# Transposed loads, zeroing by DMA, accumulator copies on VectorE and a split return of reciprocals in a fused attention and state-space kernel

## The chip, the core and the metric

The kernel runs on one core of a Trainium2 chip. The metric is the device time of one execution in microseconds, as the median of several runs. The span in a profile is the time from the first to the last instruction of one profiled execution, which is a little shorter.

## What is computed

Two branches over the same token count (2048) and width (448), mixed by a gate. Only one input, `A_x`, feeds both.

```python
g = sigmoid((x * gate_w).sum(-1))                 # one gate per token
# branch A: attention, 16 query heads of 28, one shared key/value head
q, k, v = x @ wq, x @ wk, x @ wv
a = (softmax(q @ k.T / sqrt(28)) @ v) @ wo
# branch B: diagonal state space, 256 complex states per channel, as a long convolution
dt = exp(log_dt); A = A_re + 1j*A_im
K[d, l] = Re( sum_n C[d, n] * exp(dt*A[d, n]*l) * dt*B[d, n] )
b = causal_conv(x, K) + x * Dskip                 # per channel, by FFT in the reference
out = g * a + (1 - g) * b
```

Inputs and output are bfloat16.

## The kernel before

Every operation is recorded first by `Prog.op` (L99) or `Prog.dma` (L134), with an engine, an assumed duration in ns, the keys it reads and writes, and a priority `pr` (lower is more urgent). `Prog.schedule` (L148) then simulates the engines with these durations and writes down one fixed order for each engine; `emit` (L257) turns the keys into semaphore waits. So a changed duration, priority or dependency moves instructions on all engines, and each engine follows its order strictly: whatever stands behind a waiting instruction waits too. `fill` (L624) adds matmuls that multiply by zero wherever the order leaves TensorE idle, to keep its clock up.

**Head.** `loads` (L487) brings x in four quarters of 512 tokens (`lx`, L492), six parameter arrays as raw rows (`lraw`, L499), and the weights, nearly all from the queue of SyncE. In `prep_x` (L553) TensorE transposes each quarter in two halves (L565), ScalarE evicts one half (L574) and VectorE the other (L576); the keys follow (L582), are copied by ScalarE (L588), and VectorE takes their largest magnitude (L591). The maximum over all four quarters (L602) goes into a bound `Wb` (L604) that the query projection uses (`qproj`, L806, with its second product at L825 and its copy at L828), so no score can be computed before the last quarter has come through. `prep_params` (L712) transposes the parameters on TensorE (`trans`, L732) and turns them into seeds of the state tables with VectorE (L750 to L756) and ScalarE (sines at L757 and L758, exponentials at L762 and L764). `sload` (L793) moves the first block's seeds to `sz` and `sw` by DMA. Contractions over the 448 columns of x are cut into four pieces of 112 partitions.

**Body.** `main` (L1162) walks through 1024 score tiles of 128 keys by 512 queries, in sets of three and two in turn. For each set TensorE computes scores (`qk`, L1181), ScalarE takes the exponential of the whole set (L1205) into a ring of 15 tiles, and two sets later TensorE multiplies four tiles with the values (`pv`, L1214) into one PSUM bank, `psB`. After 64 tiles a group of four heads for 512 queries is complete: `norm` (L1066) copies the bank to `acc` on ScalarE (L1074; the last two groups on VectorE), which frees it for the next group. GpSimd then moves the 2048 denominators to `denT` (L1080), VectorE inverts them (L1082), GpSimd writes them to a scratch tensor (L1085) and reads them back broadcast over the partitions into `rdenB` (L1086), and VectorE multiplies (L1088).

Between these, for branch B, VectorE squares "master" powers (`masters`, L831) and builds tables from them (`tables`, L876), TensorE contracts them to the convolution kernel (`kgen`, L938, matmuls at L959), and GpSimd stores it (slots `kw0` and `kw1`). SyncE loads it back as Toeplitz tiles of 1072 KB (`tload`, L991), and TensorE convolves (`conv`, L1000, matmuls at L1015, inverse transforms at L1037), adding into the output buffer `O` (L1045). There are 28 convolutions and 112 such loads.

**Tail.** After the last exponential the last group is normalised with matmuls instead of DMA (L1091 onwards) and `tail` (L1124) makes the last output tiles and stores everything.

Of the kernel before, what the change touches and what calls it, by code (L numbers as in the profile page):

```python
# [11 lines left out]
P = 128  # L12
# [19 lines left out]
HALVES = (13,)  # L32
NTR = 5
# [47 lines left out]
class Prog:  # L81
# [52 lines left out]
    def dma(self, pairs, desc, slot, rd=(), wr=(), pr=0, eng="sp", slow=False, extra=0):  # L134
        kw = dict(allow_slow_non_contiguous=True) if slow else {}

        def fn(e):
            return [e.dma_start(o, i, **kw) for o, i in pairs]  # L138
        nd, size = desc
        o = self.op(eng, fn, nd * (30.0 + 0.03 * size if size < 1500 else 105.0 + 0.022 * size) / 16.0 * 1.1, rd, wr, pr)  # L140
        o.slot, o.ndma, o.extra = slot, len(pairs), extra
        prev = self.slots.get(slot)
        if prev is not None:
            o.deps[prev] = 1
        self.slots[slot] = o.i
        return o
# [210 lines left out]
class Kernel:  # L357
# [18 lines left out]
    def build(self):  # L376
        nc = self.nc
        with self.es:
            self.pg = Prog(nc, self.es)
            self.alloc()  # L380
            self.consts()
            self.loads()
            self.prep_x()
            self.prep_params()
            self.prep_gate()
            self.main()
            self.pg.schedule()
            self.fill()
            with nc.Block() as block:
                self.pg.emit(block)  # L390

    def alloc(self):
# [26 lines left out]
        self.tslots = [(self.T, s * TW, ["tpdone", "rawdone"]) for s in range(NTR)]  # L419
# [26 lines left out]
    def consts(self):  # L446
# [13 lines left out]
        dm(self.Wq.v(0, P, 28, [[32, 64], [1, 4]]), 0.0, 300, ["Wq"])  # L460
# [22 lines left out]
        dm(V(self.Wo, 0, NT * D), 0.0, 810, ["Wo"], 5)  # L483
        for q in range(4):
            dm(V(self.O, q * 4 * D, 4 * D), 0.0, 800, [("O", q)], 5)

    def loads(self):  # L487
# [4 lines left out]
        def lx(q):  # L492
            pg.dma([(self.xst.v(0, P, q * 4 * D, [[1, 4 * D]]), dram(x, q * 4 * P * D, [[4 * D, P], [1, 4 * D]]))],
                   (128, 3584), f"x{q}", wr=[("xst", q)])
# [4 lines left out]
        def lraw(k):  # L499
            pg.dma([(raw.v(0, DT, k * 1024, [[1, 1024]]), dram(ins[names[k]], 0, [[1024, DT], [1, 1024]]))],  # L500
                   (112, 2048), f"raw{k}", wr=[("raw", k)])
# [3 lines left out]
        pg.dma([(self.dtb.v(0, P, 0, [[1, D]]), dram(ins["B_log_dt"], 0, [[0, P], [1, D]]))], (128, 896), "ldt", wr=["dt"], eng="act")  # L505
        lx(0)
        lraw(0)
        for k, (w, n) in enumerate((("A_wk", DH), ("A_wv", DH), ("gate_w", 1))):
            pg.dma([(wks.v(0, DT, 112 * k, [[n, 4], [1, n]]), dram(ins[w], 0, [[n, DT], [DT * n, 4], [1, n]]))],
                   (448, 2 * n), f"wk{k}", wr=[("wks", k)], eng="act", slow=True)  # L510
        for q in range(1, 4):
            lx(q)
        pg.dma([(wst.v(0, DT, 0, [[D, 4], [1, D]]), dram(ins["A_wq"], 0, [[D, DT], [DT * D, 4], [1, D]]))],
               (448, 896), "wq", wr=["wqs"])
        lraw(1)
        pg.op("dve", lambda e: e.tensor_copy(self.Wk.v(0, DT, 0, [[32, 16], [1, DH]]),
                                             wks.v(0, DT, 0, [[DH, 4], [0, 4], [1, DH]])), 300, rd=[("wks", 0)], wr=["Wk"], pr=-0.6)
        pg.op("dve", lambda e: e.tensor_copy(self.Wq.v(0, DT, 0, [[32, 64], [1, DH]]),
                                             wst.v(0, DT, 0, [[DH, 64], [1, DH]])), 620, rd=["wqs"], wr=["Wq"], pr=-0.5)
        pg.op("dve", lambda e: e.tensor_copy(self.Wv.v(0, DT, 0, [[32, 4], [1, DH]]), wks.v(0, DT, 112, [[DH, 4], [1, DH]])),  # L520
              180, rd=[("wks", 1)], wr=["Wv"], pr=0.1)
        pg.op("dve", lambda e: e.tensor_copy(self.Wv.v(0, DT, 28, [[32, 4]]), wks.v(0, DT, 224, [[1, 4]])),
              100, rd=[("wks", 2)], wr=["Wvg"], pr=0.1)
        rs = self.U.rs
        for k, (h, p0, b0) in enumerate(((1, 16, 15), (0, 0, 15), (1, 0, 31))):
            ap = bass.AP(tensor=self.U.h, offset=h * rs + p0 * D, ap=[[2 * rs, 64], [D, 16], [1, D]])
            pg.dma([(ap, dram(x, 64 * b0 * D, [[D, 64], [-64 * D, 16], [1, D]]))],
                   (1024, 896), f"u{k}", rd=["Uz"] if p0 else [], wr=[("U", k)], pr=0.5)
        for k in range(2, 6):
            lraw(k)  # L530
        pg.dma([(self.skt.v(32 * g + 31, 1, 0, [[8, 14], [1, 8]]), dram(ins["B_Dskip"], 8 * g, [[16 * D, 1], [32, 14], [1, 8]]))
                for g in range(4)], (112, 8), "sk", rd=["skt"], wr=["skt"], pr=1, slow=True)
        w = ins["A_wo"]
        pg.dma([(self.Wo.v(32 * r, DH, 0, [[D, 4], [1, D]]), dram(w, DH * r * D, [[D, DH], [4 * DH * D, 4], [1, D]]))
                for r in range(4)], (448, 896), "wo", rd=["Wo"], wr=["Wo"], pr=2)
        pg.dma([(dram(self.KP, KH + 1024, [[4 * KW, 112], [KW, 4], [1, 64]]), self.kstg.v(0, 112, 0, [[64, 4], [1, 64]]))],
               (448, 128), "pad", rd=[("kst", 0, 0), ("kst", 1, 0)], wr=["pad"], pr=3)
# [15 lines left out]
    def prep_x(self):  # L553
        pg = self.pg
        xst, xT, kT = self.xst, self.xT, self.kT
        sm = self.small
        for q in range(4):
            for hp in range(2):
# [3 lines left out]
                def mm(e, q=q, hp=hp, t=t, o=o):  # L562
                    for Tl in range(2):
                        for k in range(4):
                            r = e.matmul(t.v(0, DT, o + 512 * Tl + 128 * k, [[1, 128]]),  # L565
                                         xst.v(0, P, (4 * q + k) * D + (2 * hp + Tl) * DT, [[1, DT]]),
# [3 lines left out]
                dst = xT.v(0, DT, 2048 * q + 1024 * hp, [[512, 2], [4, 128], [1, 4]])  # L570
                src = t.v(0, DT, o, [[512, 2], [1, 128], [128, 4]])
# [5 lines left out]
            b = 4  # L577
            t, o = self.bank(b)

            def mk(e, q=q, t=t, o=o):  # L580
                for T in range(NT):
                    r = e.matmul(t.v(0, P, o, [[1, 512]]), self.Wk.v(0, DT, T * P, [[1, P]]),  # L582
                                 xT.v(0, DT, 2048 * q + 512 * T, [[1, 512]]),
# [11 lines left out]
            def mv(e, q=q):  # L595
                for kt in range(4 * q, 4 * q + 4):
                    for T in range(NT):
                        r = e.matmul(self.psB.v(0, P, 32 * kt, [[1, 29]]), xT.v(0, DT, 2048 * q + 512 * T + 128 * (kt - 4 * q), [[1, 128]]),
                                     self.Wv.v(0, DT, T * 32, [[1, 29]]), start=(T == 0), stop=(T == 3), tile_position=(0, 0))
                return r  # L600
            pg.op("pe", mv, 900, rd=["Wv", "Wvg"] + self.xk(q), wr=[("b", 6)], pr=0.5)
# [12 lines left out]
              rd=[("b", 6), "vz"], wr=["gt"], pr=0.4)  # L614
# [97 lines left out]
    def prep_params(self):  # L712
# [7 lines left out]
        tt = lambda j: spot[j][0].v(0, P, spot[j][1], [[D, 2], [4, DT], [1, 4]])  # L720
        tc = lambda j: spot[j][0].v(0, P, spot[j][1], [[D, 2], [16, 2 * NC], [1, 16]])
        K = lambda j: ("tp", j)
        dtb = self.dtb.v(0, P, 0, [[0, 2], [4, DT], [1, 4]])
# [3 lines left out]
        dtp2 = self.rdenB.v(0, P, 0, [[0, 2], [4, DT], [1, 4]])  # L727
        pg.op("act", lambda e: e.activation(dtf, d1, AF.Exp), 600, rd=["dt"], wr=[("acc", 0)], pr=-1)
        pg.op("dve", lambda e: e.tensor_copy(d1, dtf), 300, rd=[("acc", 0)], wr=["dt"], pr=-0.4)
        pg.op("dve", lambda e: e.tensor_scalar(dtp, d1, 1.0 / TWO_PI, None, ALU.mult), 300, rd=["dt"], wr=["rd"], pr=-0.4)  # L730

        def trans(k, pr):  # L732
            t_ = self.grp()
            X = ("rx", k)

            def mm(e):
                for half in range(2):
                    for T in range(4):
                        r = e.matmul(t_.bv(0, P, half * D + DT * T, [[1, DT]]),
                                     raw.v(0, DT, k * 1024 + T * NM + 128 * half, [[1, 128]]),  # L740
                                     self.ident.v(0, DT, 0, [[1, DT]]), is_transpose=True, tile_position=(0, 0))
                return r
            pg.op("pe", mm, 700, rd=[("raw", k), "id"], wr=[X, "rawdone"], pr=pr, lock=t_)
            return t_, X
# [3 lines left out]
        def vt(o, a, b, op, rd, wr, pr, **kw):  # L748
            f = lambda a: a.bv(0, P, 0, [[D, 2], [1, DT], [DT, 4]]) if isinstance(a, Grp) else a
            pg.op("dve", lambda e: e.tensor_tensor(o, f(a), b, op), ns, rd=rd, wr=wr, pr=pr, **kw)  # L750
        p0, k0 = trans(0, -0.4)
        vt(tt(1), p0, dtp2, ALU.mult, [k0, "rd"], [K(1)], -0.4, unlock=p0)
        pg.op("dve", lambda e: e.tensor_scalar(t(2), t(1), MAGIC, None, ALU.add), 660, rd=[K(1)], wr=[K(2)], pr=-0.4)
        pg.op("dve", lambda e: e.scalar_tensor_tensor(t(1), t(2), -MAGIC, t(1), ALU.add, ALU.subtract), ns,
              rd=[K(1), K(2)], wr=[K(1)], pr=-0.4)
        pg.op("dve", lambda e: e.scalar_tensor_tensor(t(2), t(1), -1.0, t(1), ALU.mult, ALU.max), ns, rd=[K(1)], wr=[K(2)], pr=-0.4)  # L756
# [3 lines left out]
        p1, k1 = trans(1, 0.15)  # L760
        vt(tt(0), p1, dtb, ALU.mult, [k1, "dt"], [K(0)], 0.2, unlock=p1)
        pg.op("act", lambda e: e.activation(t(5), t(0), AF.Exp), 2230, rd=[K(0)], wr=[K(5)], pr=0.5)  # L762
# [537 lines left out]
```

## Time and profile before

| what | value |
|---|---|
| time, median of 3 runs | 541.87 us (540.47 to 544.5) |
| span of the profiled execution | 539.0 us |
| first exponential starts | 26.74 us |
| last exponential ends | 527.73 us |
| exponentials | 410 instructions, ScalarE |
| copies of `psB` on ScalarE | 14 |
| copies of `psB` on VectorE | 1 whole (L1076), 2 halves (L1095) |
| Toeplitz loads | 112 of 1072 KB, 11.0 us from issue to landing |

In the profile, PE is TensorE's matmuls, PEld its weight loads, DVE VectorE, ACT ScalarE, POOL GpSimd and SP SyncE. A line of the groups gives code line, engine, operation, what is written from what, shapes and count; then busy time and the mean of one; then idle time of the engine just ahead of them, with what ended it. `<-` in a DMA line reads "destination from source". The clock is TensorE's, 1.00 at full speed.

### The profile page before, as it was taken

To read this page: it belongs to the slowest core of one execution; us is meant where nothing else is said; L and a number is where in the kernel's file an instruction comes from. 1 tells how busy PE (TensorE), PEld (TensorE's weight loads), DVE (VectorE), ACT (ScalarE), POOL (GpSimd) and SP (SyncE) were. 2 spreads that over 40 slices of the span, in tenths; PEclk is the share of its full clock that TensorE was granted. 3 is DMA by queue.
4 is the path that set the end of the run, shared out by engine and by line. 5 is a ranking of instruction groups with operands and counts; after the bars stand their busy time and mean duration, and the time that the engine had idled before them with its cause. 6 is when DMAs were issued, how large, how long until landed. Compare 5 with 4: busy or idle time off the path is not lost.

```text
span 539.0 us, 20180 instructions
## 1 busy us (share of the span) xinstructions
PE 486.4 (90%) x9186; PEld 249.5 (46%) x9186; DVE 449.5 (83%) x891; ACT 497.5 (92%) x458; POOL 102.1 (19%) x192
## 2 busy tenths in 40 slices
PE   7698999989999899888999898989999898999887
PEld 4442233235454555353555454553556355644434
DVE  7979999989999999899999999999999695331203
ACT  3799999998999999989999999999999796899992
POOL 2000002200431404012040430040042213220000
PEclk9989999998999999999999999999999796899998
DMA  8931100793398987979778989999859997999722
GB/s 235 283 121 47 37 21 7 251 347 116 118 376 300 329 358 284 351 259 386 296 240 363 327 273 348 400 351 367 343 191 356 353 380 287 348 344 392 261 88 71
DMA packets 39042, 142.89 MB, mean 265 GB/s; under 512 B 11240, under 2 KB 22032, under 8 KB 24620
## 3 DMA queue, kind: packets, MB, share of 16 engines
q1 hardware_dynamic: 28316, 135.30, 69.0%
q0 software_dynamic: 9104, 6.13, 4.4%
q8 instruction: 72, 1.18, 0.9%
q10 hardware_dynamic: 1536, 0.17, 0.3%
q14 instruction: 14, 0.11, 0.1%
HBM read 135.39 MB, written 5.74 MB: 262 GB/s over the span
## 4 chain that ended last, share of the span: by engine, by line
ACT 56%; PE 26%; DMA 8%; DVE 8%; issue 2%; ACTq 0%
ACT expT L1205 54%; PE psS L1181 7%; PE psB L1214 4%; PE psS L959 3%; PE psX L959 3%; DMA rdenB<-R_scratch 3%; PE psX L1015 3%; DMA denT<-acc 2%; DMA sz<-in_A_wv_dram 2%; PE psS L1015 2%; ACT acc L1074 1%; DMA R_scratch<-denT 1%; DVE msq L856 1%; DVE xT L576 1%; DVE tab L911 1%
## 5 line engine op out<-in xcount | busy, mean ns | idle before, releaser
L1205 ACT ACTIVATE expT<-psS 128x1536 bf16<-128x1536 f32 (+1 forms) x410 | 470.6, 1340 | 18.7 <-PE psS L1181 11.7
L1181 PE MATMUL psS<-qT,kT 32*128 32x512 bf16 x1024 | 164.3, 395 | 29.8 <-ACT expT L1205 22.3
L1214 PE MATMUL psB<-expT,vaug 128*32 128x512 bf16 x1024 | 105.1, 400 | 3.7 <-issue 3.2
L1181 PEld LDWEIGHTS psS<-qT,kT 32*128 32x128 bf16 x1024 | 39.5, 91 | 119.3 <-ACT expT L1205 97.3
L1187 PE MATMUL psB<-ident,zero 32*128 32x512 bf16 x190 | 74.9, 394 | 0.0
L911 DVE TENSOR_TENSOR tab<-tab,mbf 128x256 bf16<-128x256 bf16 (+5 forms) x75 | 69.6, 928 | 1.2
L1015 PE MATMUL psX<-T,U 128*18 128x128 bf16 (+7 forms) x1920 | 54.7, 243 | 4.2 <-issue 3.2
L1214 PEld LDWEIGHTS psB<-expT,vaug 128*32 128x32 bf16 x1024 | 26.4, 93 | 64.8 <-issue 62.8
L1015 PEld LDWEIGHTS psX<-T,U 128*18 128x18 bf16 (+7 forms) x1920 | 47.6, 161 | 15.1 <-issue 11.2
L640 PE MATMUL psB<-ident,zero 128*32 128x512 bf16 (+3 forms) x728 | 48.6, 336 | 0.0
L138 POOL DMA_DIRECT2D KP_scratch<-xT x64 | 34.4, 544 | 43.6 <-ACT xT L972 43.6
L138 POOL DMA_DIRECT2D KP_scratch<-kstg x63 | 34.1, 549 | 34.2 <-ACT kstg L972 32.5
L959 PE MATMUL psX<-tab 128*32 128x64 bf16 x960 | 39.7, 293 | 0.3 <-DVE tab L935 0.3
L913 DVE TENSOR_TENSOR tmp<-tab,mbf 128x256 bf16<-128x256 bf16 (+4 forms) x62 | 39.6, 638 | 0.0
L1015 PE MATMUL psS<-T,U 128*32 128x128 bf16 (+7 forms) x1344 | 39.3, 243 | 0.0
L138 POOL DMA_DIRECT2D denT<-acc x15 | 10.8, 717 | 146.8 <-ACT acc L1074 137.9
L1015 PEld LDWEIGHTS psS<-T,U 128*32 128x32 bf16 (+7 forms) x1344 | 34.0, 161 | 8.9 <-issue 6.9
L959 PE MATMUL psS<-tab 128*32 128x64 bf16 x832 | 35.3, 293 | 0.0
L138 POOL DMA_DIRECT2D R_scratch<-denT x15 | 8.6, 576 | 138.7 <-DVE denT L1082 59.2
L930 DVE TENSOR_TENSOR tab<-tab,tmp 128x2048 bf16<-128x2048 bf16 x28 | 33.5, 1219 | 0.2
L959 PEld LDWEIGHTS psX<-tab 128*32 128x32 bf16 x960 | 30.3, 138 | 6.7 <-issue 3.8
L959 PEld LDWEIGHTS psS<-tab 128*32 128x32 bf16 x832 | 26.4, 137 | 7.4 <-issue 5.4
(179 smaller groups left out, 599.1 us busy)
## 6 DMA issues: line engine op xcount, KB each, us to landing
T<-KP_scratch SPq DMA_DIRECT2D x102, 1072.0 KB, 11.0
xT<-KP_scratch SPq DMA_DIRECT2D x7, 1072.0 KB, 10.5
rdenB<-R_scratch POOLq DMA_DIRECT2D x15, 256.0 KB, 12.4
tab<-KP_scratch SPq DMA_DIRECT2D x3, 1072.0 KB, 8.8
U<-in_A_x_dram SPq DMA_DIRECT2D x3, 896.0 KB, 15.4
tab<-in_A_x_dram SPq DMA_DIRECT2D x4, 448.0 KB, 7.5
SZ_scratch<-tab SPq DMA_DIRECT2D x1, 1344.0 KB, 8.6
out_dram<-O SPq DMA_DIRECT2D x3, 448.0 KB, 3.8
```

What stands on the lines that cost most here:

```text
L138: return [e.dma_start(o, i, **kw) for o, i in pairs]
L576: pg.op("dve", lambda e, d=dst, s=src: e.tensor_copy(d, s), 1130, rd=[("b", b)], wr=[key], pr=-0.6)
L640: r = e.matmul(t.v(32 * j, 32, bo, [[1, 128 * m]]), self.zero.v(0, P, 0, [[1, 32]]), self.ident.v(0, P, 0, [[0, m], [1, P]]), start=not ac ...
L911: vo(lambda e, dst=dst, src=src, mr=mr: e.tensor_tensor(dst, src, mr, ALU.mult), 2 * n, done + mk(lv), kr + ki)
L913: vo(lambda e, src=src, mi=mi, w=w, n=n, tb=tb, to=to: e.tensor_tensor(tb.v(0, P, to, [[n, 2], [cw, w], [1, cw]]), src, mi, ALU.mult), 2 * ...
L930: vo(lambda e, h=h: e.tensor_tensor(tab.v(0, P, FM + 32 * h, [[64, 2], [EW, 32], [1, 32]]), tab.v(0, P, lo + 31 * EW + 64 * h, [[BLK, 2], ...
L959: r = e.matmul(G.v(32 * g, 32, 64 * jj, [[1, 64]]), tab.v(0, P, lo + comp * BLK + 32 + o, [[EW, 32]]), tab.v(0, P, fo, [[mo - fo, 2], [EW, ...
L1015: r = e.matmul(ps.v(32 * j, 32 - 2 * n, 128 * k, [[1, 128]]), self.U.v(0, P, 2 * n * D + 4 * gi + j, [[D, 32 - 2 * n]]), tb.v(0, P, to + j ...
L1181: r = e.matmul(self.psS.v(0, P, 512 * (bo + k), [[1, 512]]), kT.v(32 * h, 32, 128 * kt, [[1, 128]]), qT.v(32 * h, 32, 512 * (i % 2), [[1, ...
L1187: r = e.matmul(self.psB.v(0, P, 0, [[1, 512]]), self.zero.v(32 * h, 32, 0, [[1, P]]), self.ident.v(32 * h, 32, 0, [[0, 4], [1, P]]), start ...
L1205: pg.op("act", lambda e: e.activation(expT.v(0, P, 512 * es, [[1, n]]), self.psS.v(0, P, 512 * bo, [[1, n]]), AF.Exp, scale=SQ), 50 + n / ...
L1214: r = e.matmul(self.psB.v(32 * h, 32, 0, [[1, 512]]), vaug.v(0, P, 32 * kt, [[1, 32]]), expT.v(0, P, 512 * (t % RING), [[1, 512]]), start= ...
```

## The change

Its parts are meant to shorten the start, to take work off ScalarE, and to speed up the way back of the reciprocals.

- **Transposed loads.** Quarters 0 and 1 of x and all six parameter arrays are read with transposing DMA (`tdma`) directly into their final layout. Quarters 2 and 3 come first, as before, and still go through TensorE. The contraction pieces are now 128 partitions; the fourth overlaps the third by 64 rows, which are zero in the weights. The weights' padding is done in several smaller copies, and Wq is loaded in two parts.
- **Zeroing by DMA.** The buffers `Wo` and `O` are zeroed by five transfers from the zero tile, not by VectorE. These and other loads that are needed later are recorded in a function of their own, `late`; keys make a later VectorE operation wait for them (`("mb", 10)` and `sqq`).
- **Seeds.** The first block's seeds go to `sz` and `sw` by VectorE copies, not by DMA. The last master (k = 10) and the last square (level 4) are written directly as bfloat16, which saves their copies.
- **Accumulator copies.** The copies of `psB` after each group move from ScalarE to VectorE.
- **Reciprocals.** They come back in four transfers of 32 partitions each, not in one of 128.
- Assumed durations and priorities in the planner change with these; the assumed cost of a DMA descriptor under 1500 bytes changes from 30 + 0.03 per byte to 12 + 0.036.

```diff
+DP = dict(x2=-1.00, x3=-0.95, raw0=-0.90, x0=-0.85, raw1=-0.80, wq0=-0.75, x1=-0.70, wq1=-0.65)
...
+    def tdma(self, pairs, ns, slot, wr, pr):
+        o = self.dma(pairs, (1, 1), slot, (), wr, pr)
+        o.fn = lambda e: [e.dma_start_transpose(a, b) for a, b in pairs]
+        o.ns = ns
+        return o
...
-        dm(V(self.Wo, 0, NT * D), 0.0, 810, ["Wo"], 5)
-        for q in range(4):
-            dm(V(self.O, q * 4 * D, 4 * D), 0.0, 800, [("O", q)], 5)
...
+            pg.tdma([(self.xT.v(0, P, 2048 * q, [[512, 3], [1, 512]]), dram(x, 512 * q * D, [[D, 512], [1, 384]])),
+                     (self.xT.v(0, P, 2048 * q + 1536, [[512, 1], [1, 512]]), dram(x, 512 * q * D + D - P, [[D, 512], [1, P]]))],
+                    2900, f"x{q}", wr=self.xk(q), pr=DP[f"x{q}"])
...
-            pg.dma([(raw.v(0, DT, k * 1024, [[1, 1024]]), dram(ins[names[k]], 0, [[1024, DT], [1, 1024]]))],
-                   (112, 2048), f"raw{k}", wr=[("raw", k)])
+            pg.tdma([(raw.v(0, P, k * 1024, [[D, 2], [1, D]]), dram(ins[names[k]], 0, [[NM, D], [1, NM]]))],
+                    1270, f"raw{k}", wr=[("raw", k)], pr=DP.get(f"raw{k}", 0))
...
+        for k, (b, n, keys, pr) in enumerate(((self.Wo, 14, ["Wo"], 1.9), *((Sub(self.O, 4 * D * q), 14, [("O", q)], 5 + q) for q in range(4)))):
+            pg.dma([(b.v(0, P, 0, [[P, n], [1, P]]), self.zero.v(0, P, 0, [[0, n], [1, P]]))], (P * n, 256), f"z{k}", rd=["zero", ("mb", 10)], wr=keys, pr=pr)
...
+            pg.op("dve", lambda e: e.tensor_copy(self.sz.v(0, P, 0, [[BW, 3], [1, w]]), self.seed.v(0, P, o, [[W2, 3], [1, w]])), 270,
+                  rd=["sz0", "sz1", "sq"], wr=["sre", "sim", "sqq"] + [("wks", k) for k in range(3)], pr=0.9)
...
+                if k == 10:
+                    dv(lambda e: e.scalar_tensor_tensor(last(1), f[0], 2.0, f[1], ALU.mult, ALU.mult), w, keys(9) + tp, [("mb", 10)])
+                    dv(lambda e: e.tensor_tensor(last(0), f[2], f[3], ALU.subtract), w, ["msq"] + tp, [("mb", 10)])
+                    continue
...
-        if i < 14:
+        if i < 0:
             pg.op("act", lambda e: e.activation(av, self.psB.v(0, P, 0, [[1, 512]]), AF.Copy), 490, rd=[("b", 6)], wr=[ak, kb], pr=-1)
-        elif i == 14:
+        elif i < 15:
             pg.op("dve", lambda e: e.tensor_copy(av, self.psB.v(0, P, 0, [[1, 512]])), el(512), rd=[("b", 6)], wr=[ak, kb], pr=0)
...
-            pg.dma([(self.rdenB.v(0, P, 0, [[1, 512]]), dram(self.R, i * 2048, [[512, 4], [0, 32], [1, 512]]))],
+            pg.dma([(self.rdenB.v(32 * h, 32, 0, [[1, 512]]), dram(self.R, i * 2048 + 512 * h, [[0, 32], [1, 512]])) for h in range(4)],
                    (128, 2048), "rdb", rd=[("R", i)], wr=["rd"], pr=0, eng="pool", extra=4500)
```

## The prediction, made before the changed kernel was run

> **What bounds the kernel now.** I read the page first, then the busy time of each engine by stages, then the groups of ScalarE, then the timeline.
>
> ```profile
> span 539.0 us, 20180 instructions
> PE 486.4 (90%) x9186; PEld 249.5 (46%) x9186; DVE 449.5 (83%) x891; ACT 497.5 (92%) x458; POOL 102.1 (19%) x192
> ...
> ACT 56%; PE 26%; DMA 8%; DVE 8%; issue 2%; ACTq 0%
> ```
>
> ScalarE (ACT) is busiest and holds most of the chain, but the average hides three stages, cut here at the first exponential, near the end of VectorE's table work, and at the last exponential:
>
> ```profile
> 0.00:26.74 26.74, 18.70 (x188) 11.29 (x188) 23.09 (x41) 14.79 (x16) 3.44 (x20) 0.97 0.94 261
> 26.74:424.00 397.26, 363.93 (x7102) 182.00 (x7101) 378.90 (x744) 385.50 (x353) 82.56 (x144) 0.98 0.73 263
> 424.00:527.73 103.73, 95.91 (x1860) 51.25 (x1857) 42.91 (x97) 96.17 (x87) 16.14 (x28) 0.92 0.84 299
> 527.73:539.00 11.27, 7.88 (x40) 4.96 (x40) 4.62 (x11) 1.09 (x2) 0.00 (x0) 0.85 0.13 42
> ```
>
> Columns: stretch, length, then busy PE, PEld, DVE, ACT, POOL, clock, DMA share, GB/s. Head: 26.7 us, DMA 94% and VectorE 86% busy, no exponential. Body: 397.26 + 103.73 = 501.0 us, of which ScalarE is idle (397.26 - 385.50) + (103.73 - 96.17) = 19.3 us; VectorE is 95% busy in its first part. Tail: 11.3 us. So the time is head + ScalarE's work + its 19.3 us of waits + tail.
>
> ```profile
> L1205 ACT ACTIVATE expT<-psS 128x1536 bf16<-128x1536 f32 x205 | 318.4, 1553 | 12.6 <-PE psS L1181 11.7 <-PE psB L1187 0.7
> L1205 ACT ACTIVATE expT<-psS 128x1024 bf16<-128x1024 f32 x204 | 230.3, 1129 | 6.0 <-PE psB L1187 5.8
> L1074 ACT ACTIVATE acc<-psB 128x512 f32<-128x512 f32 x14 | 8.7, 621 | 0.2 <-PE psB L1214 0.2
> ...
> 431.96 0.60 ACT L1074 ACTIVATE acc<-psB 128x512 f32<-128x512 f32 x1
> 432.45 10.50 ACT L1205 ACTIVATE expT<-psS 128x1536 bf16<-128x1536 f32 x9
> ```
>
> Instructions overlap on ScalarE: the copy shows 0.60 us, but the next exponential starts 0.49 us after it. That is what a copy costs.
>
> The head ends like this:
>
> ```profile
> 20.27 1.04 PE L582 MATMUL psS<-xT,expT 112*128 112x512 bf16 x4
> 23.17 0.63 DVE L591 TENSOR_REDUCE small<-kT 128x1 f32<-128x512 bf16 x1
> 25.34 0.69 DVE L828 CAST qT<-psX 128x512 bf16<-128x512 f32 x1 [0.59 <-PE psX L825]
> 26.74 2.37 ACT L1205 ACTIVATE expT<-psS 128x1536 bf16<-128x1536 f32 x2 [1.61 <-PE psS L1181]
> ```
>
> From the last key projection to the first exponential are 6.5 us of strict sequence: no score exists before the maximum over all four quarters of x.
>
> **What the Trainium skill says.** "VectorE: DVE Perf Modes", section "The three transpose paths", gives a transposing DMA 1309 ns for one 128x128 bf16 block, and about 90% of DMA bandwidth; the two are far apart, and no run here yet shows one. "DMA: Bandwidth & Descriptors", section "Latency and other measured facts", has 261 GB/s for transposes with a non-contiguous middle dimension. The same page, section "Why a DMA increments its semaphore by 16 and not by 1", says a transfer is spread over the largest count up to 16 that divides the slowest dimension of both sides. The reciprocals' return has 4 on its source side, so 4 engines; after the change, 32 and 32, so 16. The trace agrees with few engines:
>
> ```profile
> T<-KP_scratch SPq DMA_DIRECT2D x102, 1072.0 KB, 11.0
> rdenB<-R_scratch POOLq DMA_DIRECT2D x15, 256.0 KB, 12.4
> denT<-acc POOLq DMA_DIRECT2D x15, 8.0 KB, 6.3
> ...
> 119.51 0.69 DVE L1088 TENSOR_TENSOR onT<-acc,rdenB 128x512 bf16<-128x512 f32 x1 [1.51 <-DMA rdenB<-R_scratch]
> ```
>
> A quarter of the bytes takes longer than a table load. "TensorE: Matmul & The Clock Gate", section "Part 1: The HAM clock gate", has the clock halve after an idle window of about 3.4 us. The trace agrees in kind: cut into 3.41 us steps, the clock is below 1.00 around 123, 362, 420 and 447 us, each after a pause of TensorE of 1.2 to 2.7 us.
>
> **The change, part by part.**
>
> *Copies to VectorE.* Fourteen L1074 copies leave ScalarE: 14 x 0.49 to 0.51 = 7.0 us less in the stage where it is the bound. VectorE gets 14 x 0.61 (spacing of its 512-column operations, as 440.15 to 440.76) = 8.5 us. It loses five memsets (5 x 0.81 = 4.05), two of four xT copies (2 x 1.2 = 2.4) and, per block of states, the last master copy and square copy (4 x 0.5 = 2.0), and gets some 0.5 for the seed copies: net about zero, so VectorE stays near 95%, not above. A new wait: the next value product needs psB free, and the copy stands behind table operations of up to 2.2 us in VectorE's order; TensorE has its scores queued behind that product, and ScalarE waits for these. The ring of 15 exponential tiles is 15 x 0.456 = 6.8 us deep, so most of such a delay is absorbed; I allow 0 to 6 us in all and take 2.
>
> *Return in four transfers.* GpSimd issues three more per group, 15 x 3 x 0.7 = 32 us more of an engine that is 19% busy; the last of the four starts 2.1 us later. On 16 engines each carries a quarter as much, so landing falls from 12.4 us to between 6 (what 8 KB takes) and 12; I take 8. What it is worth on the path is the 1.51 us wait of VectorE above and the pauses of TensorE that followed it, with 2.1 us of ScalarE idle in 120 to 140: 0 to 2.1 us less, I take 2.1.
>
> *Head.* Two of four x quarters and all parameters arrive transposed: 32 of 64 TensorE transposes of x, all 48 of the parameters, and four PSUM evictions go, none of them now the long pole; memsets leave VectorE; the weights' padding becomes a few copies. What counts is when the last quarter of x lands. Ahead of it in the queue, itself included: 2 x 0.459 MB of x plain, 2 x 0.524 of x (overlapping columns) and 2 x 0.229 of parameters transposed, 0.115 of Wq: 2.54 MB. At the head's 261 GB/s all of it takes 9.7 us and lands, with 0.8 before the first issue and 2.0 for a small transfer (denT at 61 us), at 12.5; at half that rate for the 1.51 MB transposed, at 18.3; at 1309 ns for each of 46 blocks of 128x128, past 60. I take 15.5. Adding the 6.5 us of sequence gives 22.0, and the parameter work of VectorE and ScalarE stands ahead of the last maximum in their orders, so 22.5: 4.2 us less. Ends: 19.0 and 24.8, and far beyond.
>
> *Zeroing by DMA.* Five transfers of 0.459 MB in 256-byte pieces: 8,960 pieces, on ScalarE's queue 1,536 small packets took 0.3% of 16 engines' span, or 17 ns each, so some 9.5 us of all engines, behind 2.75 MB of U. The first block's last master on VectorE now waits for them, a later square for the last paddings, and the first copy of psB is queued behind both. They should land at 45 to 55 us, just when needed: 0 to 5 us, I take 2. The seeds' copy on VectorE replaces a 2.5 us transfer, in the shade.
>
> *End.* In TensorE's order the last inverse transforms of the convolution now follow all scores, where 11 of 1024 score tiles followed them before. The reserve of about 5 us is gone; table loads already fill DMA to 1.00 for 480 to 500 us at 373 GB/s. I allow 0 to 8 us and take 0.4.
>
> Sum: head 22.5; body 501.0 - 7.0 - 2.1 + 2 + 2 + 0.4 = 496.3; tail 11.3; span 530.1. The measured median lies 541.87 - 539.0 = 2.9 above the span: **533.0 us**.
>
> **The rivals.**
> - *The copies give nothing back* (chance 0.20). VectorE, 95% busy, or DMA becomes the bound: ScalarE's 7 us turn into waits for psB and for tables. For it: the 95%, and the end without reserve. Against: VectorE's total does not grow. Body 501, head 22.5: 541.9 - 4.2 = 537.7.
> - *All of it, and fewer pauses* (0.19). Transposes at plain rate (head 19.0), 7 us of copies, and a third of the 19.3 us of waits gone since no return is slow: 541.9 - 7.7 - 7 - 5 = 522.
> - *Transposes are slow* (0.13, the other side). At 60 GB/s the 1.51 MB take 25 us, with 4 for the rest and 2.8 of latency: last quarter at 32, first exponential at 38.5, 11.8 later than now; less the 7: 546.7. Nothing in this trace speaks against it but that loads run at 261 GB/s.
>
> **How the numbers follow.** Forecast 533.0 with 0.48. The range leaves out the far slow case and the best of the good one: 522 to 543. Faster by over 1% is below 536.5: most of the forecast, the good case and a third of the first rival, 0.69; within 1%, the rest of these two, 0.18; slower 0.13.
>
> **What would show it.** The first exponential near 22.5 us, with the last quarter of x landed near 15.5; no copy on ScalarE between exponentials and its idle after the first exponential still 17 to 22 us; the return landing in about 8 us; VectorE at 94 to 97% up to its last table. Wrong would be: a first exponential after 27 us, VectorE idle at 45 to 60 us for the zeroing, waits of value products for the copies, or a tail longer than 12 us because the convolution comes last.

## The result, and the profile after

The changed kernel takes 528.61 us (median of 4 runs, 524.42 to 533.61) against 542.46 us (540.47 to 544.5) for the kernel before on the same chip: a ratio of 0.9719, 95% interval 0.9645 to 0.9792. It was measured twice more, beside the experiments: 531.35 us (0.9805, 0.9751 to 0.9859) and 528.60 us (0.9837, 0.9787 to 0.9886). The forecast was 533.0 with a range of 522 to 543. The forecast gain is 541.87 - 533.0 = 8.9 us; the first comparison gives 13.9, the other two, with medians of 540.63 and 538.13 us for the kernel before, 9.3 and 9.5.

Ratios leave out slow executions, more than 1.5% above the fastest of their kernel, so they are not quotients of the medians, which hold all executions; the first profile of the changed kernel fell in such an execution, and the profile shown here is that of its second measurement (`again`, the same code).

The page after, its first lines and the line on the chain of waits:

```profile
span 526.7 us, 20073 instructions
PE 483.0 (92%) x9111; PEld 243.1 (46%) x9111; DVE 452.2 (86%) x901; ACT 487.1 (92%) x442; POOL 121.6 (23%) x237
...
ACT 71%; PE 19%; DVE 4%; DMA 2%; issue 1%; another core or an unknown queue 1%; ACTq 1%
```

ScalarE lost 10.4 us of work (497.5 to 487.1), VectorE's total hardly moved (449.5 to 452.2), and "another core or an unknown queue" is a new entry in the chain. The three stages, cut as before at the first and last exponential (length, then busy PE, PEld, DVE, ACT, POOL, clock, DMA share, GB/s):

```profile
0.00:24.33 24.33, 17.78 (x153) 8.65 (x153) 20.75 (x46) 12.79 (x15) 3.47 (x20) 0.97 0.91 170
24.33:424.00 399.67, 371.07 (x7143) 181.40 (x7144) 380.74 (x738) 385.69 (x348) 97.86 (x180) 0.96 0.78 273
424.00:515.47 91.47, 86.34 (x1786) 47.97 (x1782) 45.88 (x107) 87.56 (x79) 20.28 (x37) 0.98 0.86 327
515.47:526.70 11.23, 7.84 (x40) 5.09 (x40) 4.81 (x12) 1.10 (x3) 0.00 (x0) 0.85 0.50 163
```

The head is 24.33 us (before 26.74), the body 399.67 + 91.47 = 491.1 (501.0), the tail 11.2 (11.3). In the body ScalarE is busy 385.69 + 87.56 = 473.2 us (before 481.7) and idle 17.9 (19.3). So the 12.3 us between the two profiles are 2.4 of head, 8.4 of ScalarE's work, 1.4 of its waits and 0.1 of tail. The groups of ScalarE by shape say where the waits lie:

```profile
L1231 ACT ACTIVATE expT<-psS 128x1536 bf16<-128x1536 f32 x205 | 320.6, 1564 | 20.2 <-PE psS L1207 15.3 <-remote 4.7 <-PE psX L722 0.2
L1231 ACT ACTIVATE expT<-psS 128x1024 bf16<-128x1024 f32 x204 | 232.8, 1141 | 0.4 <-PE psB L1213 0.4
```

The copies are gone from this engine, and so are the 5.8 us for `psB`. In their place stands one wait of 4.7 us for "remote", which no step of the prediction had. It comes in the first 100 us after the first exponential, where ScalarE is idle 8.3 us against 3.5 before; in the rest of the body it is idle 9.6 against 15.8.

(Lines have moved: score product L1207, exponential L1231, value product L1240, copy of `psB` L1102, multiplication by the reciprocals L1114, convolution L1041.)

### The profile page after: what moved, and what is told of

The parts are those of the page before. It is cut to its first block, busy times and chain, and to the rows that moved or that the text cites. A ratio compares the mean times of both kernels' runs of the same rounds, so it can differ in the third digit from the quotient of the medians.

```text
span 531.9 us, 20054 instructions
## 1 busy us (share of the span) xinstructions
PE 482.7 (91%) x9092; PEld 244.1 (46%) x9111; DVE 452.3 (85%) x901; ACT 488.8 (92%) x442; POOL 121.4 (23%) x237
## 3 DMA queue, kind: packets, MB, share of 16 engines
q8 instruction: 71, 1.16, 0.9%
## 4 chain that ended last, share of the span: by engine, by line
ACT 71%; PE 20%; DVE 3%; DMA 3%; issue 1%; another core or an unknown queue 1%
ACT expT L1231 70%; PE psS L1207 6%; PE psB L1240 3%; PE psX L985 2%; DMA T<-KP_scratch 2%; PE psX L1041 2%; PE psS L1041 1%; DMA tab<-in_A_x_dram 1%; PE psS L985 1%; PE psS L832 1%; PE psB L658 1%; PE psS L1166 1%; DVE xT L594 0%; ACT kstg L998 0%
## 5 line engine op out<-in xcount | busy, mean ns | idle before, releaser
L1231 ACT ACTIVATE expT<-psS 128x1536 bf16<-128x1536 f32 (+1 forms) x410 | 469.6, 1356 | 23.9 <-PE psS L1207 18.4
L1207 PE MATMUL psS<-qT,kT 32*128 32x512 bf16 x1024 | 165.4, 397 | 30.1 <-ACT expT L1231 22.9
L1240 PE MATMUL psB<-expT,vaug 128*32 128x512 bf16 x1024 | 105.3, 402 | 0.6 <-ACT expT L1231 0.3
L1207 PEld LDWEIGHTS psS<-qT,kT 32*128 32x128 bf16 x1024 | 39.5, 91 | 120.7 <-ACT expT L1231 93.5
L1213 PE MATMUL psB<-ident,zero 32*128 32x512 bf16 x188 | 73.8, 392 | 0.0
L1240 PEld LDWEIGHTS psB<-expT,vaug 128*32 128x32 bf16 x1024 | 26.3, 93 | 61.9 <-issue 58.5
L658 PE MATMUL psB<-ident,zero 128*32 128x512 bf16 (+3 forms) x728 | 50.2, 345 | 1.9 <-issue 1.9
L985 PE MATMUL psX<-tab 128*32 128x64 bf16 x1152 | 50.4, 293 | 0.1
L1041 PE MATMUL psX<-T,U 128*20 128x128 bf16 (+7 forms) x1696 | 49.6, 241 | 0.3 <-DMA T<-KP_scratch 0.2
L1041 PEld LDWEIGHTS psX<-T,U 128*20 128x20 bf16 (+7 forms) x1696 | 42.3, 162 | 12.9 <-issue 10.3
L1041 PE MATMUL psS<-T,U 128*32 128x128 bf16 (+7 forms) x1568 | 44.3, 238 | 1.9 <-issue 1.6
L139 POOL DMA_DIRECT2D rdenB<-R_scratch x60 | 30.8, 520 | 58.3 <-DMA R_scratch<-denT 51.3
L1041 PEld LDWEIGHTS psS<-T,U 128*32 128x32 bf16 (+7 forms) x1568 | 39.2, 161 | 9.9 <-issue 7.1
L985 PEld LDWEIGHTS psX<-tab 128*32 128x32 bf16 x1152 | 37.0, 138 | 10.2 <-issue 7.0
L939 DVE TENSOR_TENSOR tab<-tab,mbf 128x4096 bf16<-128x4096 bf16 x13 | 29.7, 2285 | 0.0
## 6 DMA issues: line engine op xcount, KB each, us to landing
tab<-KP_scratch SPq DMA_DIRECT2D x3, 1072.0 KB, 14.1
```

The costliest lines, as they stand in the source:

```text
L658: r = e.matmul(t.v(32 * j, 32, bo, [[1, 128 * m]]), self.zero.v(0, P, 0, [[1, 32]]), self.ident.v(0, P, 0, [[0, m], [1, P]]), start=not ac ...
L939: vo(lambda e, src=src, mi=mi, w=w, n=n, tb=tb, to=to: e.tensor_tensor(tb.v(0, P, to, [[n, 2], [cw, w], [1, cw]]), src, mi, ALU.mult), 2 * ...
L985: r = e.matmul(G.v(32 * g, 32, 64 * jj, [[1, 64]]), tab.v(0, P, lo + comp * BLK + 32 + o, [[EW, 32]]), tab.v(0, P, fo, [[mo - fo, 2], [EW, ...
L1041: r = e.matmul(ps.v(32 * j, 32 - 2 * n, 128 * k, [[1, 128]]), self.U.v(0, P, 2 * n * D + 4 * gi + j, [[D, 32 - 2 * n]]), tb.v(0, P, to + j ...
L1207: r = e.matmul(self.psS.v(0, P, 512 * (bo + k), [[1, 512]]), kT.v(32 * h, 32, 128 * kt, [[1, 128]]), qT.v(32 * h, 32, 512 * (i % 2), [[1, ...
L1213: r = e.matmul(self.psB.v(0, P, 0, [[1, 512]]), self.zero.v(32 * h, 32, 0, [[1, P]]), self.ident.v(32 * h, 32, 0, [[0, 4], [1, P]]), start ...
```

## The experiments

Ratios are to the kernel before on the same chip; those of one set (A, B, C) share a chip.

| kernel | median us, all executions | ratio, 95% interval |
|---|---|---|
| A: changed kernel (again) | 531.35 | 0.9805 (0.9751 to 0.9859) |
| A: no_copies | 540.35 | 1.0012 (0.9977 to 1.0046) |
| A: start_only | 547.75 | 1.0106 (1.0044 to 1.0167) |
| A: copies_only | 548.13 | 1.0123 (1.0075 to 1.0171) |
| B: gw_late | 529.94 | 0.9833 (0.9752 to 0.9915) |
| B: no_false_waits | 528.87 | 0.9834 (0.9754 to 0.9915) |
| B: memset_zero | 526.55 | 0.9777 (0.9704 to 0.9851) |
| B: x_plain | 545.14 | 1.0147 (1.0115 to 1.0179) |
| C: changed kernel (after_ref) | 528.60 | 0.9837 (0.9787 to 0.9886) |
| C: gate16 | 525.68 | 0.9741 (0.9687 to 0.9796) |
| C: gate_rows | 539.47 | 1.0020 (0.9993 to 1.0048) |
| C: gate_memset | 522.48 | 0.9698 (0.9644 to 0.9752) |

### The parts, taken out one after the other

`again` is the changed kernel unaltered. `no_copies` puts 14 copies back on ScalarE; `start_only` also puts the return back into one transfer; `copies_only` is the kernel before with only the copies moved.

```diff
 # no_copies, start_only
-        if i < 0:
+        if i < 14:
 # start_only as well
-dram(self.R, i * 2048 + 512 * h, [[0, 32], [1, 512]])) for h in range(4)]
+dram(self.R, i * 2048, [[512, 4], [0, 32], [1, 512]]))]
 # copies_only, in the kernel before
-        if i < 14:
+        if i < 0:
```

> The changed kernel once more, unaltered, as the yardstick for the others on the same chip and for a second trace. Expected: 528 us (524 to 533), first exponential at 24.5 us. A pause of 4.4 us in which ScalarE, VectorE and TensorE all stood still at 54 us lay in the first trace; if it belongs to the program (its waits on the zeroing transfers and paddings) it comes again, if it is an accident it doesn't, and the span is about 4 us shorter.

> The changed kernel with the accumulator copies left on ScalarE. Theory A (the copies are the largest part: 14 x 0.5 us off the engine that bounds the body): 528 + 7 = 535 us. Rival B (what VectorE's copies add in waits eats the gain, and the rest of the change does the work): 527 to 530 us.

> The changed kernel with the copies on ScalarE and the reciprocals back in one transfer: the new start, zeroing and seeds alone. Theory A: start 2.3 us earlier and nothing else, 542.5 - 2.3 = 540 us, and the return in one transfer lands in about 12 us again. Rival B (the relief of VectorE from memsets, evictions and copies, with tables ready earlier, removes waits in the body): 532 to 536 us.

> The kernel before with the accumulator copies on VectorE, nothing else. Theory A (7 us off ScalarE count wherever they are taken): 542.5 - 7 = 535.5 us. Rival B (VectorE gains 8.5 us of work without the relief that the rest of the change gives it; in TensorE's order four convolutions' inverse transforms now follow the last score, none did before): no gain or slower, 542 to 550 us, with the tail after the last exponential longer than 11.3 us.

Read upwards from `start_only`: the start with the zeroing alone is 1.1% slower than before; the split return makes that 0.1%; the copies bring it to 2.0% faster. Neither the start nor the copies make the kernel faster by themselves; the split return alone was not tried. Why the start alone is slower is not followed here; the stop described further down is part of it.

**The copies** alone are slower, though they do what was priced: the body shrinks from 501.0 to 493.3. The stages of `copies_only` around and after the last exponential show where it goes:

```profile
424.00:519.31 95.31, 86.25 (x1791) 48.03 (x1788) 50.48 (x111) 88.93 (x81) 20.33 (x36) 0.98 0.95 359
519.31:548.40 29.09, 15.00 (x331) 10.84 (x328) 8.34 (x18) 1.09 (x2) 0.70 (x1) 0.82 0.60 210
```

The tail is 29.1 us, not 11.3, with 331 matmuls in it, two whole convolutions and three inverse transforms among them, which used to lie between scores. VectorE has 459.4 us of work, 10 more than before; its last table operation starts at 472.9 us (463.1 before), and this is work and not waiting, since up to there VectorE is idle 30.3 us (30.9 before). In the tail TensorE waits for table loads three times, 1.6 to 2.1 us each; the last is issued only at 520.6 us and lands 14.1 us later. That the later tables cause the longer tail fits this, but TensorE's order changed as well, and no run separates the two.

In the changed kernel the memsets, evictions and master copies have left VectorE. The copies make its work grow there too, from 444.7 us in `no_copies` to 452.2, but this is about what it was before the change; the last table operation starts at 463.0, and the tail stays at 11.2. There the same edit is worth 540.35 - 531.35 = 9.0 us.

**The split return** is worth 1.0106 - 1.0012 = 0.9% by the ratios, some 5 us; the two intervals just touch. The issues of the return in the DMA tables of `start_only` and of `again` (KB each, us to landing):

```profile
rdenB<-R_scratch POOLq DMA_DIRECT2D x15, 256.0 KB, 9.9
```

```profile
rdenB<-R_scratch POOLq DMA_DIRECT2D x60, 64.0 KB, 4.9
```

And the wait of VectorE for it in the waits of `start_only` (us in total, times, longest):

```profile
DVE onT L1114 <- DMA rdenB<-R_scratch: 10.6, 2, 8.2
```

In the kernel before that wait is 2.2 us, in `no_copies` one of 7.1, in `again` none. (The profile of `start_only`, at 550.8 us, lies above its median.) How the shorter landing becomes these 5 us was not followed further. GpSimd pays with 60 issues of 0.52 us, and is busy 122 us of 527, up from 102.

### What stops all engines at 54 us

ScalarE's wait for "remote" is no wait of ScalarE alone. Windows of `again` (columns as above):

```profile
50.00:52.00 2.00, 1.88 (x32) 0.50 (x28) 2.00 (x7) 2.00 (x3) 0.00 (x0) 1.00 3.44 105
52.00:54.00 2.00, 1.89 (x30) 0.52 (x22) 1.97 (x4) 1.65 (x2) 0.00 (x0) 1.00 0.19 2
54.00:56.00 2.00, 1.18 (x10) 0.31 (x7) 2.00 (x4) 0.00 (x0) 0.00 (x0) 1.00 0.74 10
56.00:58.00 2.00, 0.00 (x0) 0.00 (x0) 0.05 (x1) 0.00 (x0) 0.00 (x0) 0.74 0.39 15
58.00:60.00 2.00, 0.17 (x3) 0.11 (x3) 0.00 (x0) 1.68 (x2) 0.00 (x0) 0.50 0.66 45
```

ScalarE stops first, then TensorE, then VectorE. The two DMA columns count a packet whole where it starts: those that start from 52 us on carry only 2 to 15 GB/s, and the 3.44 says that those that start at 50 to 52 us take 3.44 x 2.00 = 6.9 us per DMA engine. The clock then stays at 0.50 until about 67 us. It is in every profile of set A that has the new start, and neither in the kernel before nor in `copies_only`. The timeline of `again` names the transfers around it (start, duration, `xN` issues):

```profile
47.56 0.88 SPq L139 DMA_DIRECT2D R_scratch<-gt  x1
48.50 0.50 SPq L139 DMA_DIRECT2D SW_scratch<-tab  x1
49.04 9.28 SPq L139 DMA_DIRECT2D Wo<-in_A_wo_dram  x4
58.32 2.37 ACT L1231 ACTIVATE expT<-psS 128x1536 bf16<-128x1536 f32 x2 [4.67 <-remote]
59.85 0.60 SPq L139 DMA_DIRECT2D gtT<-R_scratch  x1
```

`R_scratch<-gt` writes 512 gates to scratch, 4 bytes each; `gtT<-R_scratch` reads them back and waits for that write, so the write took up to 12.3 us (12.0 in `after_ref`, where SyncE waits 8.3 us for nothing else). In the kernel before it was issued at 31.2 us. It comes later now because other transfers of the same queue do: the zeroing and, through `sqq`, the Dskip row. Four kernels move or remove what lies near it.

```diff
 # gw_late: this transfer and its return in a function called after group 3, with
+rd=["gt", ("on", 0)]
 # no_false_waits: the keys that only order transfers are left out
-rd=["zero", ("mb", 10)]      # zeroing
+rd=["zero"]
-rd=["skt", "sqq"]            # Dskip; the same for the padding
+rd=["skt"]
 # memset_zero: as in the kernel before; the five zeroing transfers are taken out
+        dm(V(self.Wo, 0, NT * D), 0.0, 810, ["Wo"], 5)
+        for q in range(4):
+            dm(V(self.O, q * 4 * D, 4 * D), 0.0, 800, [("O", q)], 5)
 # x_plain: all four quarters of x loaded plainly and transposed on TensorE (its staging and evictions follow)
-            if q > 1:
+            if q > -1:
```

> The kernel after, with one small transfer moved: the gates on their way to scratch (512 writes of 4 bytes, issued at 47.6 us) are now issued just before the first Toeplitz load, at about 100 us. Theory A (the descriptors of these 4-byte writes, ahead in the same queue, hold back what the engines need and so cause the standstill of all engines at 54 to 58 us): the standstill is gone from there, ScalarE's idle time in the first 100 us after the first exponential falls from 8.3 to 3 to 4 us, and the time from 531 to 523 to 527 us; if the same happens at 100 us instead, the time stays. Theory B (the other small transfers beside it, Dskip, padding and the output weights, or the zeroing): the standstill stays where it was and the time at 529 to 533 us.

> The kernel after, without the keys that only order transfers: the zeroing no longer makes the last master wait, and the Dskip and padding transfers no longer stand behind the seeds. Theory A (4-byte gate writes cause the standstill): a standstill follows wherever these writes now stand, about 5 us after their issue, time 528 to 533. Theory B (Dskip and padding): it moves forward with them or vanishes in the head, time 523 to 527. Theory C (a wait of VectorE for the zeroing costs something that the profile does not name): VectorE is earlier at 50 us and the time falls by 1 to 2 us.

> The kernel after, with Wo and O zeroed by five VectorE memsets as before the change. Theory A (the zeroing transfers were needed to relieve VectorE, 5 x 0.81 = 4.05 us, and had no cost of their own): VectorE has 4 us more, the last convolutions end later, tail 11 to 15 us, time 531 to 536. Theory B (the zeroing transfers, 13 to 15 us of SyncE's issue and 8,960 pieces of 256 bytes, push the small transfers to 45 to 50 us and so cause the standstill at 54 us): no standstill, ScalarE idle 3 to 4 us in the first 100 us, time 524 to 528 in spite of the memsets.

> The kernel after, with quarters 0 and 1 of x loaded plainly and transposed on TensorE, as quarters 2 and 3 are; the parameters stay transposed by DMA. Theory A (the transposing loads of x were no limit; the order of VectorE's work, busy from 11 us on, sets the first exponential): two more evictions of 1.2 us on VectorE and two of 1.0 on ScalarE, first exponential at 25 to 27 us, against 24.3, time 531 to 535. Theory B (the transposing loads are what holds the start, since each half of x occupies SyncE's queue for 2.8 us and the last one lands only after 17 us): first exponential at 21.5 to 23.5 us, time 527 to 530.

The ratios of `gw_late` and `no_false_waits` are those of the changed kernel, and that of `memset_zero`, within the time of its theory B, doesn't decide, since the gates' write moved forward with the rest; what tells the theories apart is where the stop lies:

| kernel | gates written at, us | read back at, us | what stops, for how long and until when |
|---|---|---|---|
| before | 31.2 | 45.8 | nothing clear |
| memset_zero | 34.3 | 46.5 | VectorE 2.0 to 46.3 (for the padding, see below) |
| x_plain | 41.8 | 52.5 | ScalarE 2.2 to 52.5, TensorE nearly idle from 51 |
| no_false_waits | 42.6 | 58.7 | ScalarE 2.7 to 53.7, TensorE nearly idle from 52 |
| changed kernel | 47.6 | 59.9 | ScalarE 4.7 to 58.3, all from 56 |
| gw_late | 83.9 | 99.1 | ScalarE 2.3 to 94.1 ("remote") |

The 4-byte write takes 10.8 to 12.3 us where SyncE stands waiting for it; in the kernel before, `no_false_waits` and `gw_late` the read stands behind other issues, and 14.6 to 16.1 us are upper bounds. With the new start something stops 6 to 10 us after its issue, wherever that lies. In `memset_zero` this is an ordinary wait: the profile names the store of the padding (`KP_scratch<-kstg`), which was issued 0.7 us ahead of the gates in the same queue and landed 12.7 us later, against 2.4 in `again`. (In the kernel before the write stops nothing that the timeline shows. SyncE issues nothing between 31.6 and 43.6 us there, so little stands behind it; that this is why it is harmless is not shown.) The output weights, the padding and the zeroing keep no such distance: in `gw_late` they stay at 42 to 50 us, and ScalarE runs without a gap through 54 to 60. So the theory of the small write stands, and a mere shift is no cure: in `gw_late` ScalarE is idle 8.6 us in its first 100.

The packets of other transfers show the hold-up. First line: those of SyncE's queue that start at 50 to 52 us in `again` (packets, MB, share of 16 engines over the stretch), 0.9 us each. Second: the same stretch of `gate16`, the kernel described next, 0.06 us each. Third and fourth: the one packet of the instruction queue that starts within 0.5 us, at 91.0 us in `gw_late` and at 48.0 in `no_false_waits`; they take 4.0 and 6.0 us, where the packets of this queue take 1.1 on average in `again`.

```profile
q1 hardware_dynamic: 123, 0.21, 343.9%
q1 hardware_dynamic: 407, 0.36, 75.0%
q8 instruction: 1, 0.02, 50.1%
q8 instruction: 1, 0.02, 74.6%
```

The cleanest test changes nothing but the size of the pieces. In `gate16` the instructions of every engine are the same, in the same order; the gates lie in scratch in another order, so the last quarter of tokens is mixed with gates that are not its own. `gate_rows` takes the gates from a transposed copy of 1 - g that TensorE makes for the other branch anyway, `gate_memset` adds the memsets.

```diff
 # gate16
-dram(self.R, 15 * 2048, [[1, P], [128, 4]])
+dram(self.R, 15 * 2048, [[4, P], [1, 4]])
 # gate_rows, gate_memset, in prep_gate (the old gw and gr are taken out of prep_x)
+        pg.dma([(dram(self.R, 15 * 2048, [[128, 4], [1, 128]]), ogT.v(12, 4, 0, [[1, 128]]))], (4, 512), "gw", rd=[("acc", 0)], wr=["GT"], pr=4, slow=True)
+        pg.dma(..., (128, 64), "gr", rd=["GT"], wr=["gtT"], pr=4)
+        pg.op("dve", lambda e: e.tensor_scalar(gT, gT, -1.0, 1.0, ALU.mult, ALU.add), 80, rd=["gtT"], wr=["gtT"], pr=4)
```

> The kernel after, every instruction of every engine in the same order, but the gates go to scratch as 128 pieces of 16 bytes where they were 512 pieces of 4; they arrive in another order, so the last quarter of tokens gets wrong gates. Theory A (these 4-byte writes hold back what the engines need): from issue to the read that waits for them 3 to 6 us, where the kernel after has 12.3; no standstill at 54 us, ScalarE idle 3 to 5 us in its first 100 us against 6.3 and 8.3; 5 to 6 us less than the kernel after in the same call. Theory B (something else that lies near them, the output weights or the padding): unchanged, standstill and time as in the kernel after.

> The kernel after, with the gates written from the transposed copy that TensorE makes anyway for the other branch: 4 pieces of 512 bytes in the place of 512 of 4, and one VectorE operation of 0.1 us that turns 1 - g back into g. Theory A: no standstill, 5 to 6 us less than the kernel after, 523 to 526 if that has 529 to 531; the planner's order changes as well, which can cost or bring some 3 us by itself. Theory B: standstill as before.

> As gate_rows, and Wo and O zeroed by VectorE memsets. If the zeroing transfers cost nothing themselves, 4 us more of VectorE make it 0 to 4 us slower than gate_rows; if they have a cost beside the standstill, it is 2 to 4 us faster, near 521 to 523.

> The changed kernel unaltered, as the measure for the other three: 527 to 532 us, standstill of 4 to 5 us at 54 to 59 us.

The windows of `gate16` at the same place:

```profile
52.00:54.00 2.00, 1.89 (x33) 0.52 (x22) 1.97 (x5) 2.00 (x3) 0.00 (x0) 1.00 0.30 68
54.00:56.00 2.00, 1.75 (x14) 0.52 (x11) 2.00 (x4) 2.00 (x3) 0.00 (x0) 1.00 0.03 8
56.00:58.00 2.00, 1.38 (x15) 0.40 (x12) 1.90 (x5) 2.00 (x3) 0.42 (x1) 1.00 0.00 0
58.00:60.00 2.00, 1.87 (x27) 0.54 (x26) 2.00 (x4) 2.00 (x4) 0.43 (x1) 1.00 0.11 5
```

and its DMA table:

```profile
R_scratch<-gt SPq DMA_DIRECT2D x1, 2.0 KB, 2.0
```

The same 2 KB land in 2.0 us, ScalarE is busy without a gap, and its idle time in the first 100 us is 1.5 us, against 8.1 in the changed kernel of that set. That the write in 4-byte pieces causes the stop is shown. What the stop costs is less sure: 5 to 6 us were expected, the medians lie 2.9 us apart and the ratios 1.0%, some 5 us, and the two intervals overlap by a hair. (The profile of `gate16`, at 521.42 us, is the lowest of its executions.)

All three kernels without 4-byte pieces have no stop. `gate_memset`, at 522.48 us (518.08 to 524.12), beats the changed kernel of its set (527.85 to 533.08) in every run, and so both kernels of this case. `gate_rows`, though, is 11 us slower than the changed kernel, with its stop gone. Why, is the next point.

### A wait for the copies after all

ScalarE's longest wait in `gate_rows` ends at 283 us. Its timeline (lines of other work left out):

```profile
265.11 0.40 PE L1242 MATMUL psB<-expT,vaug 128*32 128x512 bf16 x4
...
273.15 2.81 PE L1043 MATMUL psS<-T,U 128*32 128x128 bf16 x96 [1.29 <-DVE qT L846]
...
281.03 0.69 DVE L1116 TENSOR_TENSOR onT<-acc,rdenB 128x512 bf16<-128x512 f32 x1
281.96 0.69 DVE L1104 COPY acc<-psB 128x512 f32<-128x512 f32 x1
...
282.70 1.02 PE L1242 MATMUL psB<-expT,vaug 128*32 128x512 bf16 x12 [0.23 <-DVE acc L1104]
...
283.35 1.46 ACT L1233 ACTIVATE expT<-psS 128x1536 bf16<-128x1536 f32 x1 [13.01 <-PE psB L1242]
```

No value product runs from 265.5 to 282.7, since `psB` is full and its copy comes at 281.96. By the code, the copy goes to one of two halves of `acc`, which the multiplication L1116 of an earlier group must have read first; that one has a low priority and a slack of 4 us in the planner, and stands behind tables in VectorE's order, right ahead of the copy. TensorE does not even wait: the planner saw the copy come late and filled the gap with convolution. ScalarE, 15 tiles ahead, ran dry and waited 13.0 us. `x_plain` has the same event at 407 us; its groups of ScalarE by shape:

```profile
L1231 ACT ACTIVATE expT<-psS 128x1536 bf16<-128x1536 f32 x205 | 320.2, 1562 | 15.4 <-PE psS L1207 15.1
L1231 ACT ACTIVATE expT<-psS 128x1024 bf16<-128x1024 f32 x204 | 232.2, 1138 | 13.2 <-PE psB L1240 10.6 <-PE psB L658 2.2 <-PE psB L1213 0.3
```

In the changed kernel the copies that stand alone in the timeline start 0.05 to 1.6 us after the last value product of their group, and ScalarE never waits for one. The dependence on `acc` is older than the change; new is that copy and multiplication stand in one engine's order. So the copies on VectorE bring a chain, multiplication, half of `acc`, copy, `psB`, that the order of this kernel happens not to hit and that of two near relatives does. The chain is read from the code and the order of the timeline; that a third half of `acc` or an earlier multiplication would remove it was not tried.

`x_plain` missed both its theories: first exponential at 27.78 us, later than either said, and 545.14 us. Transposing x by DMA is worth 3.4 us at the start in these profiles. How much of the rest of its loss is this one wait, and how much the later order, is not separated; its profile, at 538.69 us, is also the lowest of its 20 executions.

`memset_zero` and `gate_memset` show that the zeroing by DMA brings nothing measurable here: with 4 us more on VectorE and a first exponential 2 us later (26.2 and 26.4), they lie some 3 us below their nearest relatives that zero by DMA (526.6 to 528.9 and 529.9; 522.5 to 525.7), with intervals that overlap. `gate_memset` against `gate_rows`, for which the expectation was written, decides nothing because of the wait above.

## Why the prediction was right, and where not

- **Copies, 7.0 us off ScalarE.** Right: its work in the body fell by 8.4 us, 14 copies of 0.49 to 0.51 among it; the other 1.4 us were not traced. That VectorE's total ends where it was before was the condition, and `copies_only` fits it: where it ends 10 us higher, the gain is lost in the tail. So the first rival describes the edit alone, not the whole change. VectorE was 94% busy up to its last table, as forecast.
- **Copies, a wait for `psB`, 0 to 6 us, 2 taken.** About 0 in this kernel. The mechanism was right, but the ring of 15 tiles was said to absorb most of such a delay and 6 us to be the end; 10.6 and 13.0 us occur. The wait is not for table operations of 2.2 us but for `acc`.
- **Return.** Landing 8 us forecast, 4.9 measured; worth 2.1 us forecast, some 5 measured between two kernels with the new start. The step took the one wait visible before as the whole worth. The Trainium skill, "DMA: Bandwidth & Descriptors", section "Why a DMA increments its semaphore by 16 and not by 1", pointed the right way: 9.9 to 12.4 us in one transfer, 4.9 to 6.0 for each quarter. All four together take longer: some 6.5 us from the first issue, an estimate from three issues of 0.52 and the 4.9.
- **Head, 22.5 us.** The step that failed is the landing of the last quarter of x at 15.5 us, worked out from bytes and rates, and with it that the key product follows at once. The timeline of `again`:

```profile
11.73 2.84 SPq L151 DMA_TRANSPOSE xT<-in_A_x_dram  x2
...
16.87 1.04 PE L832 MATMUL psX<-xT,Wq 128*128 128x512 bf16 x4 [1.66 <-DVE Wq L541]
...
18.50 1.03 PE L600 MATMUL psS<-xT,expT 128*128 128x512 bf16 x4
...
19.59 1.08 DVE L754 TENSOR_TENSOR tab<-mbf,T 128x896 f32<-128x896 f32 x1
20.58 0.68 DVE L609 TENSOR_REDUCE small<-kT 128x1 f32<-128x512 bf16 x1
...
22.93 0.68 DVE L844 CAST qT<-psX 128x512 bf16<-128x512 f32 x1
...
24.33 1.45 ACT L1231 ACTIVATE expT<-psS 128x1536 bf16<-128x1536 f32 x1 [3.24 <-PE psS L1207]
```

  The last quarter is only issued from 11.73 to 14.57 us, because transposing loads hold SyncE's queue: 1.2 to 1.8 us for a parameter array, 2.8 for a quarter of x and 5.6 for the first. They land after 3.3 to 7.8 us, far from the slow rival, and from the 1309 ns per block that the prediction quotes: by an estimate from it, the 12 blocks of the larger load of a quarter would take 15.7. The two loads of the last quarter land 3.4 and 4.4 us after their issues, the second of which starts at 13.3: at 16.7 to 17.7 us, 1.2 to 2.2 later than forecast. The key product comes later still, at 18.50, since it stands behind a query product that waited 1.66 us for a copy of weights. From there, where it does not wait for the data, to the first exponential are 5.8 us, close to the 6.5 taken; two L754 of VectorE stand inside, ahead of the maximum and of the query copy.
- **Zeroing, 2 us.** No wait for it: VectorE runs on at 50 us. That it moves the gates' write back was in none of the steps.
- **End, 0.4 us.** Right: the tail is 11.2 us with the convolutions last.
- **What was missing.** The gates' write, moved from 31.2 to 47.6 us, stops ScalarE, then TensorE and VectorE, and the clock halves. The prediction read in the profile that transfers moved and looked only at what waits for them. A warning was in the Trainium skill: "DMA: Bandwidth & Descriptors", section "Rules for kernel authors", says that a strided last dimension lowers to one descriptor per element; here 512 pieces took 12.0 us and 128 pieces 2.0.

So the total is right by its main term, but that it is within 4.4 us is partly luck, since misses cancel. In the profile of `again` (span 526.7, forecast 530.1) the head gave 1.8 us less than forecast and ScalarE's work 1.4 more; its waits are 17.9 us where the steps add up to 21.6 (19.3 - 2.1 + 2 + 2 + 0.4), although the stop, which no step had, takes 4.7 of them. The 2.9 us from span to median mixed two executions: the profiled one took 540.75, 1.8 above its span, as in `again` (528.48).

## What to carry to other kernels

When a change moves work to another engine, price the total of that engine first: the same 14 copies cost 1.2% where they took VectorE from 449.5 to 459.4 us and brought some 9 us where other parts had relieved it first and they took it from 444.7 to 452.2. List every transfer whose place in its queue moves, with the size of its pieces, and not only those that someone waits for. And follow a copy that frees a bank to its destination: the wait that costs may be for the buffer it writes, not for the engine it runs on.

## What was not expected of the hardware

- A 2 KB write in 512 pieces of 4 bytes takes 10.8 to 12.3 us, packets of other transfers that start behind it are held up, and ScalarE, which has nothing to do with it, stops for 2.2 to 5.5 us in most kernels with the new start. How it stops the engines is not shown. The Trainium skill, "Runtime: NRT & Kernel Launch", section "Instruction fetch mechanics", says that each engine's sequencer fetches its program by DMA in pages of 16 KiB; the profile of `again` agrees with 71 packets and 1.16 MB on the queue "instruction", 16.3 KB each. Fetches held up behind the small pieces would fit a wait for "remote" that no semaphore explains. The traces go part of the way: in `gw_late` and `no_false_waits` one such packet takes 4.0 and 6.0 us, and in the changed kernel none starts between 47.5 and 60.5 us, where `gate16` has two, at 52.5 and 55.5. But ScalarE goes on at 58.3 us, ahead of the next one, so which engine waits for which fetch stays open.
- In the kernel before, the clock fell after pauses of TensorE of 1.2 to 2.7 us, shorter than the 3.4 us that the prediction quotes.
- A transposing load costs its queue far more than a plain one: 2.8 us for 512 tokens of x, where a plain quarter was issued in about 0.4 us.
